# Block-sparse attention with top-2 experts: score products paired the other way round, and the row maximum carried by one transposed tile and a row copy

## Chip, cores and metric

One Trainium2 core of a chip with eight. The metric is the device time of one execution in microseconds (us); lower is better. Three executions of the kernel before took 1046.15, 1049.36 and 1059.47 us.

## What is computed

The reference first computes attention for 4 batches x 8 heads, 768 positions, head size 64, under a mask of blocks of 32 positions (neighbours, first and last block, three sampled blocks for each block of queries). Its rows then go through a top-2 mixture of 8 experts. Cut to what matters here:

```python
scores = 0.125 * (q @ k.T)                 # for each batch and head
scores = where(mask, scores, -1e9)
scores = scores - scores.max(-1)
attn = exp(scores); attn = attn / (attn.sum(-1) + 1e-9)
x = attn @ v                               # then rows of all heads, 3072 x 512
# router, top 2 of 8 experts, relu(x @ w1[e]) @ w2[e]
```

## The kernel before

The attention half (class Attention) runs over 32 heads, two heads to a group g, 16 groups. The 768 positions are T = 6 tiles of 128. A step n is one tile of 128 keys of one head (192 steps): `exp(n, x)` makes the scores of 128 keys against 384 queries (x = 0, 1) in PSUM and takes their exponential on ACT (L257), `halve` rescales them on DVE (L262), and `av`, three steps later, multiplies them with v on PE (L288).

q and k are 32-bit and are used as a sum of two 16-bit halves, a high part (qh, kh) and the remainder (ql, kl). A score is kh qh + kl qh + kh ql. Two products of up to 128 rows give it, and the rows above the first 64 carry the rest of the arithmetic:

- L255: `k1` (rows kh, kl) with `q1` (rows qh, qh).
- L256: `k2` (rows kh, 24 rows of the mask, two rows of the constant 64) with `q2` (rows ql, 24 rows eh that say in which block a query lies, a row -m/64, a constant row).

The row maximum m is needed ahead of the exponential. `max_mm` (L227) multiplies the upper part of `q3` (qh, eh) with `k2` (kh, mask), 88 rows, and `max_red` (L234) reduces on DVE. This work runs up to 11 steps ahead of the exponentials. When the last tile of a head is reduced, `max_end` writes -m/64 into the tile qb (L241, DVE) and one step later (`Q2LATE`) SP issues the transpose of the head's whole qb, six blocks of 128x128, into `q2` (L243).

The operands of a group are prepared two groups ahead by `split`, in the order of the table SPLITAT: casts of k and q to the high parts on ACT (L192, L196), remainders on POOL a step later (L194, L198), the transposes of ka (k1) and qa (q3) on SP at steps 5 and 6 of the 12 steps of a group (L181), the copy of kh from k1 to k2 at step 8 (L205), and two copies of qh from q3 to both halves of q1 at step 9 (L208, L209). The mask and constant rows of k2 never change: they lie in three buffers that groups use in turn.

All transposes and these copies are DMAs issued by SP, which issues in program order and stops at the first one whose semaphore isn't reached. On the same queue go, for each group, a transpose of the group's attention rows for the router (L495, x to r_xT) and their way to DRAM (L497, x_rows). ACT issues the loads of q, k and v (L160) and, in steps 20 to 48, eight stores of zeros over the output (L988, 768 KB each). The prologue `start` does the same for group 0 with SP transposes of each head, and the masks are built by `masks`, `blank` and `blocks`.

After the attention come the expert products, which the change doesn't touch.

Of the kernel before, what the change touches and what calls it, by code (L numbers as in the profile page):

```python
# [10 lines left out]
F16 = mybir.dt.float16  # L11
# [8 lines left out]
P = 128  # L20
# [24 lines left out]
class Attention:  # L45
# [27 lines left out]
    def open(self, ctx, early):  # L73

        tc, nc, G, T = self.tc, self.nc, self.G, self.T
        pool = lambda c, name, bufs, **kw: c.enter_context(tc.tile_pool(name=name, bufs=bufs, **kw))
        self.const = pool(ctx, "aconst", 1, side="right")
        self.tp = pool(ctx, "atp", 3, side="right")
        self.pp = pool(ctx, "app", self.PPB, side="right")
        self.pi = pool(ctx, "api", 3, side="right")  # L80
        self.sm = pool(ctx, "asm", 4, side="right")
        self.xp = pool(ctx, "axp", 2, side="right")
        self.ps_e = pool(ctx, "ps_e", 3, space=PSUM)
        self.ps_m = pool(ctx, "ps_m", 2, space=PSUM)
        self.ps_o = pool(ctx, "ps_o", 1, space=PSUM)
        self.natp = pool(ctx, "anat", 1, side="right")
        self.raw = pool(early, "araw", 2)
        self.nat = [tuple(self.natp.tile([P, G, T, P], F16, name=f"{n}{i}") for n in ("ka", "qa", "qb"))
                    for i in range(2)]
        self.k2 = [self.natp.tile([P, G, T, P], F16, name=f"k2{i}") for i in range(3)]  # L90

        self.vx = [self.natp.tile([P, G, T, self.D + 1], F16, name=f"vx{i}") for i in range(3)]
        self.vb = [self.natp.tile([P, G, T, self.D + 1], F16, name=f"vb{i}") for i in range(3)]
        self.vl = [self.natp.tile([P, G, T, self.D], F16, name=f"vl{i}") for i in range(3)]
        for t, w in zip(self.vx + self.vb, [VS / XS] * 3 + [VS / XS * LOW] * 3):
            nc.gpsimd.memset(t[:, :, :, self.D:], w)

    def masks(self, mi, sb):
# [9 lines left out]
        self.kb = mi.tile([P, G, T, P], F16, name="kb")  # L108
        nc.gpsimd.memset(self.kb[:, :, :, 64:], 0.0)
        nc.gpsimd.memset(self.kb[:, :, :, 64 + NB:66 + NB], 64.0)  # L110
        self.blank(0)
        nc.vector.tensor_scalar(rowi, rowi, 5, None, op0=ALU.arith_shift_right)
        rowb = mi.tile([P, T], F32, name="rowb")
        nc.vector.tensor_copy(rowb, rowi)
        rb = rowb[:, :, None].to_broadcast([P, T, NB])
        eh = mi.tile([P, T, NB], F32, name="eh")
        nc.vector.tensor_tensor(eh, bc(ei, NB), rb, op=ALU.is_equal)
        self.eh = eh
        self.blocks(0, 1)
        t1 = mi.tile([P, T, NB], F32, name="t1")  # L120
        nc.vector.tensor_tensor(t1, bc(ei, NB), rb, op=ALU.subtract)
        al = mi.tile([P, T, NB], F32, name="al")
# [15 lines left out]
            nc.vector.tensor_tensor(al, al, t3[:, :, j], op=ALU.add)  # L138
        for g in range(G):
            nc.vector.tensor_scalar(self.kb[:, g, :, 64:64 + NB], al, 0.0, -BIG, op0=ALU.is_equal, op1=ALU.mult)  # L140

    def blank(self, i):
        ka, qa, qb = self.nat[i]
        self.nc.gpsimd.memset(qa[:, :, :, 64 + self.NB:], 0.0)
        self.nc.gpsimd.memset(qb[:, :, :, 64 + self.NB:], 0.0)
        self.nc.gpsimd.memset(qb[:, :, :, 65 + self.NB:66 + self.NB], LNROW)

    def blocks(self, i, k):
        for g in range(self.G):
            self.nc.vector.tensor_scalar(self.nat[i][k][:, g, :, 64:64 + self.NB], self.eh, 2.0 ** 15, None, op0=ALU.mult)  # L150

    def load(self, g, eng=None, names="kq"):
        b, h0 = divmod(g * self.G, self.H)
# [30 lines left out]
    def split(self, g, part, h=None):  # L184

        nc, D, G, T = self.nc, self.D, self.G, self.T
        r = self.st[g]
        ka, qa, qb = self.nat[g % 2]
        kx, qx = r["k"], r["q"]
        hs = slice(0, G) if h is None else slice(h, h + 1)  # L190
        if part == 0:
            nc.scalar.activation(ka[:, hs, :, 0:D], kx[:, hs], AF.Copy)  # L192
            self.later(1 if self.now else 0,
                       lambda: nc.gpsimd.tensor_sub(ka[:, hs, :, D:], kx[:, hs], ka[:, hs, :, 0:D]))  # L194
        elif part == 1:
            nc.scalar.activation(qa[:, hs, :, 0:D], qx[:, hs], AF.Copy)  # L196
            self.later(1 if self.now else 0,
                       lambda: nc.gpsimd.tensor_sub(qb[:, hs, :, 0:D], qx[:, hs], qa[:, hs, :, 0:D]))  # L198
        elif part == 2:
            self.xpose(r, "k1", ka)  # L200
        elif part == 3:
            self.xpose(r, "q3", qa)
        elif part == 4:
            r["k2"] = self.k2[g % 3]
            nc.sync.dma_start(r["k2"][0:D], r["k1"][0:D])  # L205
        elif part == 5:
            q1 = self.new(r, "q1")
            nc.sync.dma_start(q1[0:D], r["q3"][0:D])  # L208
            nc.sync.dma_start(q1[D:], r["q3"][0:D])  # L209

    def where(self, n):
        hh, i = divmod(n, self.T)
# [6 lines left out]
    def max_mm(self, n):  # L219
        g, h, t = self.where(n)  # L220
        r = self.st[g]
        K = 64 + self.NB
        if t == 0:
            r["m", h] = self.sm.tile([P, self.T], F32, name="m")
        pm = self.ps_m.tile([P, 2, 512], F32, name="pm")
        for c in range(2):
            self.nc.tensor.matmul(pm[:, c, 0:384], r["q3"][0:K, h, t, :], r["k2"][0:K, h, 3 * c:3 * c + 3, :],  # L227
                                  start=True, stop=True)
        self.st["pm", n] = pm

# [5 lines left out]
    def max_end(self, n):  # L236
        g, h, t = self.where(n)
        r = self.st[g]
        if t == self.T - 1:
            qb = self.nat[g % 2][2]  # L240
            self.nc.vector.tensor_scalar(qb[:, h, :, 64 + self.NB], r["m", h], -1.0 / 64.0, None, op0=ALU.mult)  # L241
            d = r["q2", h] = self.tp.tile([P, self.T, P], F16, name="q2", bufs=2)
            self.later(self.Q2LATE, lambda: self.nc.sync.dma_start_transpose(  # L243
                out=d, in_=qb[:, h].rearrange("p t c -> p (t c)")))

    def exp(self, n, x):
        nc, T = self.nc, self.T
        g, h, c = self.where(n)
        r = self.st[g]
        if x == 0:  # L250
            self.st["p32", n] = self.pi.tile([P, T, P], I32, name="p32")
        p32 = self.st["p32", n]
        t = slice(3 * x, 3 * x + 3)
        pe = self.psum()
        nc.tensor.matmul(pe[:, 0:384], r["k1"][:, h, c, :], r["q1"][:, h, t, :], start=True, stop=False)  # L255
        nc.tensor.matmul(pe[:, 0:384], r["k2"][:, h, c, :], r["q2", h][:, t, :], start=False, stop=True)  # L256
        nc.scalar.activation(p32[:, t].rearrange("p t c -> p (t c)"), pe[:, 0:384], AF.Exp, scale=0.125)  # L257

    def halve(self, n):
# [61 lines left out]
    def start(self, mi):  # L321
# [7 lines left out]
            for nm, src in (("k", self.k), ("q", self.q)):  # L329
                nc.sync.dma_start(r[nm][:, h], src[0, h].rearrange("(p t) d -> p t d", p=P))  # L330
        self.masks(mi, sb)
        ka, qa, qb = self.nat[0]
        q3, k1 = self.new(r, "q3"), self.new(r, "k1")
        r["k2"] = self.k2[0]
        turn = lambda dst, src, h: nc.sync.dma_start_transpose(out=dst[:, h], in_=src[:, h].rearrange("p t c -> p (t c)"))
        for h in range(self.G):
            nc.scalar.activation(qa[:, h, :, 0:D], r["q"][:, h], AF.Copy)
            nc.scalar.activation(self.kb[:, h, :, 0:D], r["k"][:, h], AF.Copy)
            turn(q3, qa, h)
            turn(r["k2"], self.kb, h)  # L340
            self.load(1, nc.sync, "kq"[h])
        for h in range(self.G):
            nc.scalar.activation(ka[:, h, :, 0:D], r["k"][:, h], AF.Copy)
            nc.vector.tensor_sub(ka[:, h, :, D:], r["k"][:, h], ka[:, h, :, 0:D])
            nc.vector.tensor_sub(qb[:, h, :, 0:D], r["q"][:, h], qa[:, h, :, 0:D])
        nc.sync.dma_start_transpose(out=k1.rearrange("p g t c -> p (g t) c"), in_=ka.rearrange("p g t c -> p (g t c)"))
        self.blocks(0, 2)
        self.split(0, 5)
        self.blank(1)
        for n in range(self.T + self.XM):  # L350
            self.max_mm(n)
            self.max_red(n)
            if n in (self.S0, self.S0 + 1):
                self.split(1, n - self.S0)
            if n == self.S0:
                self.blocks(1, 1)
            self.max_end(n)
        self.flush()
        self.load(0, nc.scalar, "v")
        for i in range(3):  # L360
            self.vsplit(0, i)
        self.split(1, 3)
        self.split(1, 2)
        nc.sync.dma_start(self.k2[1][D:], self.k2[0][D:])
        self.split(1, 4)
        self.split(1, 5)
        self.blocks(1, 2)
        self.nmax = self.T + self.XM
        self.plan = {0: [(self.load, 2)], 3: [(self.load, 1, None, "v")], 4: [(self.load, 3)],
                     6: [(nc.sync.dma_start, self.k2[2][D:], self.k2[0][D:])]}  # L370

    def lead(self, n):
        return min(self.LM, self.T + 1 + max(0, self.NSTEP - n))
# [282 lines left out]
class Experts:  # L656
# [193 lines left out]
    def turn(self, u, c):  # L850
        m = self.rows_of(u, c)
        py = self.ps_r.tile([P, 512], F32, name="pr")
        for d in range(self.KB):
            self.nc.tensor.transpose(py[0:m, d * P:(d + 1) * P], self.yt[:, d, 0:m], self.router.ident)
        self.finish(u, c, py)
# [280 lines left out]
```

## Time and profile before

| | |
|---|---|
| median of three runs | 1049.36 us (1046.15 to 1059.47) |
| the profiled execution | 1054.67 us, its span 1052.9 us |
| mean granted clock of PE | 0.957 |
| PE busy | 897.5 us, 85% of the span |
| DVE busy | 549.4 us, 52% |
| ACT busy | 372.8 us, 35% |
| POOL busy | 340.9 us, 32% |
| DMA read and written | 156.40 MB, SP's and POOL's and ACT's queues together |
| transposes of qb, qa, ka on SP | 32, 17 and 16 |
| copies inside SBUF on SP, 192 KB each | 32 for q, 17 for k |

A line of the profile names an engine, an operation, the tiles it writes and reads, its count, its busy time and mean duration, and the idle time of the engine just ahead of it with what ended that idle time. A row of the order of time begins with its start and its duration in us. For a DMA, the row is its issue on the queue of SP or ACT; when it has landed is seen only by who waited for it. The share of DMA is that of the 16 DMA engines and can come out a little over 1.

### The profile page before, as it was taken

To read this page: it belongs to the slowest core of one execution; us is meant where nothing else is said; L and a number is where in the kernel's file an instruction comes from. 1 tells how busy PE (TensorE), PEld (TensorE's weight loads), DVE (VectorE), ACT (ScalarE), POOL (GpSimd) and SP (SyncE) were. 2 spreads that over 40 slices of the span, in tenths; PEclk is the share of its full clock that TensorE was granted. 3 is DMA by queue.
4 is the path that set the end of the run, shared out by engine and by line. 5 is a ranking of instruction groups with operands and counts; after the bars stand their busy time and mean duration, and the time that the engine had idled before them with its cause. 6 is when DMAs were issued, how large, how long until landed. Compare 5 with 4: busy or idle time off the path is not lost. (4 is left out here: it accounts for less than half of the span.)

```text
span 1052.9 us, 20575 instructions
## 1 busy us (share of the span) xinstructions
PE 897.5 (85%) x8413; PEld 531.8 (51%) x8413; DVE 549.4 (52%) x1039; ACT 372.8 (35%) x754; POOL 340.9 (32%) x399
## 2 busy tenths in 40 slices
PE   3887798888888768897797989979989999899993
PEld 1554565566566535654554445535545554454551
DVE  8787779999998945554134134133243251251220
ACT  3565556666666525432033032121131140230200
POOL 3232222552363342253360241331422422602211
PEclk9999999999999978998898999989999999999997
DMA  8999987788798518745959186194293392661200
GB/s 188 183 203 220 226 185 166 167 161 159 150 175 167 115 30 204 178 119 145 210 156 223 61 220 150 65 232 120 91 222 114 103 240 95 175 143 51 64 33 33
DMA packets 238073, 156.40 MB, mean 149 GB/s; under 512 B 172577, under 2 KB 213793, under 8 KB 237968
## 3 DMA queue, kind: packets, MB, share of 16 engines
q1 hardware_dynamic: 206816, 91.45, 42.8%
q0 software_dynamic: 14256, 39.58, 13.4%
q10 hardware_dynamic: 16896, 23.95, 8.3%
q8 instruction: 68, 1.11, 0.5%
q14 instruction: 37, 0.30, 0.1%
HBM read 79.62 MB, written 26.32 MB: 101 GB/s over the span
## 5 line engine op out<-in xcount | busy, mean ns | idle before, releaser
L257 ACT ACTIVATE p<-pe 128x384 int32<-128x384 f32 x384 | 182.4, 492 | 155.2 <-PE pe L256 128.1
L820 ACT ACTIVATE hh<-ph 128x408 f16<-128x408 f32 (+2 forms) x136 | 66.9, 493 | 378.9 <-PE ph L815 270.8
L234 DVE TENSOR_REDUCE m<-pm 128x1 f32<-128x768 f32 x192 | 181.9, 950 | 1.4 <-PE pm L227 1.4
L865 POOL DMA_INDIRECT out_dram<-y,mt x56 | 59.8, 1067 | 350.6 <-DVE y L863 258.5
L821 DVE SCALAR_TENSOR_TENSOR hl<-ph,hh 128x408 f16<-128x408 f32 (+2 forms) x136 | 76.1, 560 | 175.7 <-ACT hh L820 134.4
L227 PE MATMUL pm<-k,q 88*128 88x384 f16 x384 | 99.3, 343 | 65.3 <-DVE m L234 38.0
L262 DVE TENSOR_SCALAR p<-p 128x1536 f16<-128x1536 uint16 x192 | 115.6, 602 | 62.8 <-ACT p L257 49.7
L288 PEld LDWEIGHTS <-p 128*128 128x128 f16 x3456 | 131.6, 100 | 27.6 <-issue 6.8
L255 PE MATMUL pe<-q,k 128*128 128x384 f16 x384 | 129.8, 338 | 13.0 <-ACT p L257 6.3
L256 PE MATMUL pe<-q,k 128*128 128x384 f16 x384 | 129.1, 336 | 8.4 <-DMA q<-qb 8.2
L863 DVE SCALAR_TENSOR_TENSOR y<-py,mt,pv 128x512 f32<-128x512 f32 x48 | 36.0, 751 | 189.8 <-PE py L835 181.3
L288 PE MATMUL po<-vl,p 128*128 128x64 f16 x1152 | 126.4, 196 | 1.9 <-issue 1.9
L288 PE MATMUL po<-vb,p 128*128 128x65 f16 x1152 | 126.6, 197 | 1.5 <-issue 1.5
L288 PE MATMUL po<-vx,p 128*128 128x65 f16 x1152 | 126.2, 198 | 0.5 <-DVE p L262 0.4
L815 PE MATMUL ph<-xta,w1hb 128*128 128x408 f16 x512 | 112.4, 342 | 15.7 <-DVE hl L821 13.2
L835 PEld LDWEIGHTS <-hh 128*128 128x128 f16 x768 | 75.0, 98 | 92.1 <-issue 6.9
L815 PE MATMUL ph<-xtb,w1ha 128*128 128x408 f16 (+1 forms) x448 | 97.1, 337 | 21.6 <-DVE hl L821 16.5
L227 PEld LDWEIGHTS <-q 88*128 88x128 f16 x384 | 37.9, 100 | 120.4 <-issue 94.1
L815 PEld LDWEIGHTS <-w1ha 128*128 128x128 f16 x576 | 57.7, 101 | 61.7 <-issue 28.1
L815 PEld LDWEIGHTS <-w1hb 128*128 128x128 f16 x512 | 50.8, 99 | 57.2 <-issue 20.9
L835 PE MATMUL py<-w2ha,hh 128*128 128x512 f16 x192 | 73.8, 384 | 3.6 <-DVE y L863 3.6
L835 PE MATMUL py<-w2ha,hl 128*128 128x512 f16 x192 | 73.8, 384 | 1.7 <-issue 1.7
(172 smaller groups left out, 1398.7 us busy)
## 6 DMA issues: line engine op xcount, KB each, us to landing
wraw<-in_moe_w_dram SPq DMA_DIRECT2D x64, 512.0 KB
q<-q SPq DMA_DIRECT2D x32, 192.0 KB
raw_v<-in_v_dram ACTq DMA_DIRECT2D x16, 384.0 KB
out_dram<-zero ACTq DMA_DIRECT2D x8, 768.0 KB
x_rows<-x SPq DMA_DIRECT2D x16, 384.0 KB
raw_k<-in_k_dram ACTq DMA_DIRECT2D x14, 384.0 KB
raw_q<-in_q_dram ACTq DMA_DIRECT2D x14, 384.0 KB
k<-k SPq DMA_DIRECT2D x17, 192.0 KB
```

The lines of the kernel that those rows point to most:

```text
L227: self.nc.tensor.matmul(pm[:, c, 0:384], r["q3"][0:K, h, t, :], r["k2"][0:K, h, 3 * c:3 * c + 3, :], start=True, stop=True)
L234: self.nc.vector.tensor_reduce(self.st[g]["m", h][:, t:t + 1], pm[:, :, 0:384], axis=AX.XY, op=ALU.max)
L255: nc.tensor.matmul(pe[:, 0:384], r["k1"][:, h, c, :], r["q1"][:, h, t, :], start=True, stop=False)
L256: nc.tensor.matmul(pe[:, 0:384], r["k2"][:, h, c, :], r["q2", h][:, t, :], start=False, stop=True)
L257: nc.scalar.activation(p32[:, t].rearrange("p t c -> p (t c)"), pe[:, 0:384], AF.Exp, scale=0.125)
L262: self.nc.vector.tensor_scalar(p.rearrange("p t c w -> p (t c w)"), p32.bitcast(U16).rearrange("p t c -> p (t c)"), HC, None, op0=ALU.mult)
L288: self.nc.tensor.matmul(o, p[:, t, :, w], v, start=first and i == 0, stop=last and i == 2, skip_group_check=True)
L815: nc.tensor.matmul(ph[:, b, 0:m], w[wt][:, kb, fs], r["xt"][:, kb, a, o:o + m], start=i == 0, stop=i == last)
L820: nc.scalar.activation(hv, ph[:, b, 0:m], AF.Relu)
L821: nc.vector.scalar_tensor_tensor(self.hl[:, f, o:o + m], ph[:, b, 0:m], 0.0, hv, op0=ALU.max, op1=ALU.subtract)
L835: nc.tensor.matmul(py, h[:, f, o], w[x][:, f, :], start=i == 0, stop=i == last)
L865: nc.gpsimd.indirect_dma_start(out=self.out, out_offset=bass.IndirectOffsetOnAxis(ap=r["mt"][0:m, c, 0:1], axis=0), in_=y[0:m], in_offset= ...
```

## The change

- The first product becomes (kh, kl) with (ql, qh): one transpose of the tile qn (ql, qh) gives `q1`, and both copies of qh into it go.
- The second becomes (kh, mask, 64) with (qh, eh, -m): `q2` now holds qh, copied from the lower half of q1 (one copy), over constant rows that are kept in three buffers as those of k2 are. The maximum is taken from q2 instead of q3, which goes. The product contracts over 90 rows instead of 128.
- -m/64 is written into the first six columns of a small tile `mn`. SP transposes this one 128x128 block, and a second DMA copies its six rows into row 88 of q2 (one partition).
- The prologue follows: its q transposes go straight into q2, k1 and q1 are two transposes of 12 blocks, and the constant rows of q2 are copied into the other two buffers as those of k2 are.

```diff
-        self.nat = [tuple(... for n in ("ka", "qa", "qb")) for i in range(2)]
+        self.nat = [tuple(... for n in ("kn", "qn")) for i in range(2)]
+        self.q2 = [self.natp.tile([P, G, T, P], F16, name=f"q2{i}") for i in range(3)]
+        self.mn = [self.natp.tile([P, P], F16, name=f"mn{i}") for i in range(3)]
...
-        if part == 0:
-            nc.scalar.activation(ka[:, hs, :, 0:D], kx[:, hs], AF.Copy)
+        if part < 2:
+            src, dst, hi, lo = ((kx, kn, slice(0, D), slice(D, None)), (qx, qn, slice(D, None), slice(0, D)))[part]
+            nc.scalar.activation(dst[:, hs, :, hi], src[:, hs], AF.Copy)
             self.later(1 if self.now else 0,
-                       lambda: nc.gpsimd.tensor_sub(ka[:, hs, :, D:], kx[:, hs], ka[:, hs, :, 0:D]))
-        elif part == 1:
-            nc.scalar.activation(qa[:, hs, :, 0:D], qx[:, hs], AF.Copy)
-            self.later(1 if self.now else 0,
-                       lambda: nc.gpsimd.tensor_sub(qb[:, hs, :, 0:D], qx[:, hs], qa[:, hs, :, 0:D]))
+                       lambda: nc.gpsimd.tensor_sub(dst[:, hs, :, lo], src[:, hs], dst[:, hs, :, hi]))
         elif part == 2:
-            self.xpose(r, "k1", ka)
+            self.xpose(r, "k1", kn)
         elif part == 3:
-            self.xpose(r, "q3", qa)
+            self.xpose(r, "q1", qn)
...
         elif part == 5:
-            q1 = self.new(r, "q1")
-            nc.sync.dma_start(q1[0:D], r["q3"][0:D])
-            nc.sync.dma_start(q1[D:], r["q3"][0:D])
+            r["q2"] = self.q2[g % 3]
+            nc.sync.dma_start(r["q2"][0:D], r["q1"][D:])
...
-            self.nc.tensor.matmul(pm[:, c, 0:384], r["q3"][0:K, h, t, :], r["k2"][0:K, h, 3 * c:3 * c + 3, :],
+            self.nc.tensor.matmul(pm[:, c, 0:384], r["q2"][0:K, h, t, :], r["k2"][0:K, h, 3 * c:3 * c + 3, :],
...
-            qb = self.nat[g % 2][2]
-            self.nc.vector.tensor_scalar(qb[:, h, :, 64 + self.NB], r["m", h], -1.0 / 64.0, None, op0=ALU.mult)
-            d = r["q2", h] = self.tp.tile([P, self.T, P], F16, name="q2", bufs=2)
-            self.later(self.Q2LATE, lambda: self.nc.sync.dma_start_transpose(
-                out=d, in_=qb[:, h].rearrange("p t c -> p (t c)")))
+            mn = self.mn[(n // self.T) % 3]
+            self.nc.vector.tensor_scalar(mn[:, 0:self.T], r["m", h], -1.0 / 64.0, None, op0=ALU.mult)
+            self.later(self.Q2LATE, lambda: self.max_row(g, h, mn))
+
+    def max_row(self, g, h, mn):
+        NB, T = self.NB, self.T
+        mt = self.tp.tile([P, P], F16, name="mt", bufs=2)
+        self.nc.sync.dma_start_transpose(out=mt, in_=mn)
+        self.nc.sync.dma_start(self.st[g]["q2"][64 + NB:65 + NB, h], mt[0:T, :])
...
-        nc.tensor.matmul(pe[:, 0:384], r["k2"][:, h, c, :], r["q2", h][:, t, :], start=False, stop=True)
+        K = 66 + self.NB
+        nc.tensor.matmul(pe[:, 0:384], r["k2"][0:K, h, c, :], r["q2"][0:K, h, t, :], start=False, stop=True)
...
-        nc.sync.dma_start(self.k2[1][D:], self.k2[0][D:])
+        for t in (self.k2, self.q2):
+            nc.sync.dma_start(t[1][D:], t[0][D:])
...
-                     6: [(nc.sync.dma_start, self.k2[2][D:], self.k2[0][D:])]}
+                     6: [(nc.sync.dma_start, t[2][D:], t[0][D:]) for t in (self.k2, self.q2)]}
```

More of the change, by code (lines that the diff above doesn't have):

```diff
@@ L87, in open @@
         self.raw = pool(early, "araw", 2)
-        self.nat = [tuple(self.natp.tile([P, G, T, P], F16, name=f"{n}{i}") for n in ("ka", "qa", "qb"))
+        self.nat = [tuple(self.natp.tile([P, G, T, P], F16, name=f"{n}{i}") for n in ("kn", "qn"))
                     for i in range(2)]
         self.k2 = [self.natp.tile([P, G, T, P], F16, name=f"k2{i}") for i in range(3)]
+        self.q2 = [self.natp.tile([P, G, T, P], F16, name=f"q2{i}") for i in range(3)]
+        self.mn = [self.natp.tile([P, P], F16, name=f"mn{i}") for i in range(3)]
+        for t in self.mn:
+            nc.gpsimd.memset(t, 0.0)
         self.vx = [self.natp.tile([P, G, T, self.D + 1], F16, name=f"vx{i}") for i in range(3)]
@@ L110, in masks @@
         nc.gpsimd.memset(self.kb[:, :, :, 64 + NB:66 + NB], 64.0)
-        self.blank(0)
+        self.qb = mi.tile([P, G, T, P], F16, name="qb")
+        nc.gpsimd.memset(self.qb[:, :, :, 64 + NB:], 0.0)
+        nc.gpsimd.memset(self.qb[:, :, :, 65 + NB:66 + NB], LNROW)
         nc.vector.tensor_scalar(rowi, rowi, 5, None, op0=ALU.arith_shift_right)
@@ L117, in masks @@
         nc.vector.tensor_tensor(eh, bc(ei, NB), rb, op=ALU.is_equal)
-        self.eh = eh
-        self.blocks(0, 1)
+        for g in range(G):
+            nc.vector.tensor_scalar(self.qb[:, g, :, 64:64 + NB], eh, BIG, None, op0=ALU.mult)
         t1 = mi.tile([P, T, NB], F32, name="t1")
@@ L140, in masks @@
             nc.vector.tensor_scalar(self.kb[:, g, :, 64:64 + NB], al, 0.0, -BIG, op0=ALU.is_equal, op1=ALU.mult)
[L142 to L150, printed above, removed]
     def load(self, g, eng=None, names="kq"):
@@ L187, in split @@
         r = self.st[g]
-        ka, qa, qb = self.nat[g % 2]
+        kn, qn = self.nat[g % 2]
         kx, qx = r["k"], r["q"]
         hs = slice(0, G) if h is None else slice(h, h + 1)
-        if part == 0:
-            nc.scalar.activation(ka[:, hs, :, 0:D], kx[:, hs], AF.Copy)
+        if part < 2:
+            src, dst, hi, lo = ((kx, kn, slice(0, D), slice(D, None)), (qx, qn, slice(D, None), slice(0, D)))[part]
+            nc.scalar.activation(dst[:, hs, :, hi], src[:, hs], AF.Copy)
             self.later(1 if self.now else 0,
-                       lambda: nc.gpsimd.tensor_sub(ka[:, hs, :, D:], kx[:, hs], ka[:, hs, :, 0:D]))
-        elif part == 1:
-            nc.scalar.activation(qa[:, hs, :, 0:D], qx[:, hs], AF.Copy)
-            self.later(1 if self.now else 0,
-                       lambda: nc.gpsimd.tensor_sub(qb[:, hs, :, 0:D], qx[:, hs], qa[:, hs, :, 0:D]))
+                       lambda: nc.gpsimd.tensor_sub(dst[:, hs, :, lo], src[:, hs], dst[:, hs, :, hi]))
         elif part == 2:
-            self.xpose(r, "k1", ka)
+            self.xpose(r, "k1", kn)
         elif part == 3:
-            self.xpose(r, "q3", qa)
+            self.xpose(r, "q1", qn)
         elif part == 4:
@@ L331, in start @@
         self.masks(mi, sb)
-        ka, qa, qb = self.nat[0]
-        q3, k1 = self.new(r, "q3"), self.new(r, "k1")
-        r["k2"] = self.k2[0]
+        kn, qn = self.nat[0]
+        kb, qb = self.kb, self.qb
+        r["k2"], r["q2"] = self.k2[0], self.q2[0]
         turn = lambda dst, src, h: nc.sync.dma_start_transpose(out=dst[:, h], in_=src[:, h].rearrange("p t c -> p (t c)"))
         for h in range(self.G):
[L337 to L340, printed above, removed]
+            nc.scalar.activation(qb[:, h, :, 0:D], r["q"][:, h], AF.Copy)
+            nc.scalar.activation(kb[:, h, :, 0:D], r["k"][:, h], AF.Copy)
+            turn(r["q2"], qb, h)
+            turn(r["k2"], kb, h)
             self.load(1, nc.sync, "kq"[h])
         for h in range(self.G):
[L343 to L349, printed above, removed]
+            nc.scalar.activation(kn[:, h, :, 0:D], r["k"][:, h], AF.Copy)
+            nc.vector.tensor_sub(kn[:, h, :, D:], r["k"][:, h], kb[:, h, :, 0:D])
+            nc.scalar.activation(qn[:, h, :, D:], r["q"][:, h], AF.Copy)
+            nc.vector.tensor_sub(qn[:, h, :, 0:D], r["q"][:, h], qb[:, h, :, 0:D])
+        self.xpose(r, "k1", kn)
+        self.xpose(r, "q1", qn)
         for n in range(self.T + self.XM):
@@ L354, in start @@
                 self.split(1, n - self.S0)
-            if n == self.S0:
-                self.blocks(1, 1)
             self.max_end(n)
@@ L363, in start @@
         self.split(1, 2)
-        nc.sync.dma_start(self.k2[1][D:], self.k2[0][D:])
+        for t in (self.k2, self.q2):
+            nc.sync.dma_start(t[1][D:], t[0][D:])
         self.split(1, 4)
         self.split(1, 5)
-        self.blocks(1, 2)
         self.nmax = self.T + self.XM
         self.plan = {0: [(self.load, 2)], 3: [(self.load, 1, None, "v")], 4: [(self.load, 3)],
-                     6: [(nc.sync.dma_start, self.k2[2][D:], self.k2[0][D:])]}
+                     6: [(nc.sync.dma_start, t[2][D:], t[0][D:]) for t in (self.k2, self.q2)]}
     def lead(self, n):
```

## The prediction

> **What bounds the kernel now.** I read the page first (span, the DMA slices), then busy time by stretch, then the groups of instructions inside a stretch, then the order of time around single waits.
>
> ```profile
> span 1052.9 us, 20575 instructions
> ...
> DMA  8999987788798518745959186194293392661200
> ```
>
> The slices are 26 us each: the DMA engines are full in the first six and seldom later. The attention half is slices 0 to 15; the change touches nothing after it. I cut it into a front, a stretch in which the output is also filled with zeros, and a steady stretch.
>
> ```profile
> 22.41:66.27 43.86, 36.46 (x453) 23.66 (x452) 35.25 (x59) 25.04 (x55) 14.34 (x21) 0.96 1.01 185
> 66.27:146.41 80.14, 62.19 (x867) 43.15 (x866) 59.50 (x102) 44.87 (x101) 19.52 (x21) 0.94 1.06 223
> 146.41:343.84 197.43, 168.26 (x2608) 118.41 (x2607) 182.58 (x379) 126.48 (x289) 83.09 (x107) 1.00 0.82 162
> ```
>
> Columns: length, busy PE, PEld, DVE, ACT, POOL, granted clock, DMA share, GB/s. In the first two rows DMA is at 1.01 and 1.06, no engine above 83%. In the third DVE is busy 182.58 of 197.43 us (92%) and DMA 0.82. So **DMA bounds up to about 146 us, and DVE (with PE close) after it**. The groups of the second and third stretch say what the DMA costs:
>
> ```profile
> L257 ACT ACTIVATE p<-pe 128x384 int32<-128x384 f32 x73 | 34.9, 492 | 36.2 <-PE pe L256 33.3 <-PE pm L227 2.1 <-DVE m L234 0.2
> ...
> L256 PE MATMUL pe<-q,k 128*128 128x384 f16 x73 | 24.5, 335 | 6.8 <-DMA q<-qb 6.8
> ...
> L227 PE MATMUL pm<-k,q 88*128 88x384 f16 x73 | 18.6, 336 | 10.7 <-DMA k<-k 6.1 <-DVE m L234 4.6
> ```
>
> ```profile
> L257 ACT ACTIVATE p<-pe 128x384 int32<-128x384 f32 x205 | 97.7, 492 | 70.2 <-PE pe L256 59.3 <-PE pm L227 6.2 <-DVE r_mx L560 1.8
> ...
> L227 PE MATMUL pm<-k,q 88*128 88x384 f16 x204 | 49.7, 324 | 29.2 <-DVE m L234 22.0 <-issue 3.2 <-DMA k<-k 2.0
> ```
>
> A step has two exponentials (L257). In the fill stretch 73 of them take 80.14 us, 1.098 us each; steady, 205 take 197.43 us, 0.963 us each. At the steady pace the 73 would take 70.3 us, so the stretch loses 9.8 us, and PE's two DMA waits there add up to 12.9 us: for the late transpose that carries -m (6.8) and for the copy of kh (6.1). In the steady stretch only 2.0 us of such waits are left.
>
> **The change part by part.** For each group of two heads, TRANSPOSES go from 12 (k) + 12 (q) + 2 x 6 (ql with -m) blocks of 128x128 to 12 + 12 + 2 x 1; 192 KB COPIES from three (kh, and qh twice) to two (kh, qh); two 1.5 KB row copies are new. I price a block where a 12-block transpose is alone, and plain bytes where a zero fill runs:
>
> ```profile
> 258.30:260.30 2.00, 0.48 (x8) 0.19 (x5) 2.00 (x4) 1.25 (x3) 1.51 (x2) 1.00 1.03 195
> 69.50:70.50 1.00, 0.87 (x12) 0.60 (x12) 1.00 (x5) 0.15 (x2) 0.00 (x0) 1.00 1.07 416
> ```
>
> A block is 32.8 KB, at 195 GB/s 0.168 us of all 16 engines; 196.6 KB at 416 GB/s is 0.47 us. Saved in each group: 10 x 0.168 + 0.47 = 2.15 us.
>
> *Fill stretch.* 73 exponentials are three groups (24 each), so 6.5 us of DMA time goes. While DMA is the bound this comes off the time: **-6.5**. Bounds: 0 (the waits stay latencies) and -9.8 (the steady pace, where DVE is late next).
>
> The row is also faster here than the transpose it replaces:
>
> ```profile
> 76.28 3.10 SPq L243 DMA_TRANSPOSE q<-qb  x1
> ...
> 86.11 5.81 SPq L181 DMA_TRANSPOSE q<-qa  x1
> ```
>
> ```profile
> 87.33 0.32 PE L256 MATMUL pe<-q,k 128*128 128x384 f16 x1 [1.66 <-DMA q<-qb]
> ...
> 100.44 0.32 PE L256 MATMUL pe<-q,k 128*128 128x384 f16 x1 [2.74 <-DMA q<-qb]
> ```
>
> Under load the six blocks took 11 us from issue (76.28) to use (87.33); one block has a sixth of the packets to get through the same crowd.
>
> *Front.* The first head shows both kinds of transfer with little beside them:
>
> ```profile
> 19.12 1.21 SPq L243 DMA_TRANSPOSE q<-qb  x1
> ...
> 29.42 0.46 SPq L205 DMA_DIRECT2D k<-k  x1
> ```
>
> ```profile
> 21.90 0.48 PE L256 MATMUL pe<-q,k 128*128 128x384 f16 x1 [1.42 <-DMA q<-qb]
> ...
> 32.23 0.81 PE L227 MATMUL pm<-k,q 88*128 88x384 f16 x4 [2.21 <-DMA k<-k]
> ```
>
> Six blocks: 19.12 to 21.90 = 2.78 us. One block: five blocks less, 2.78 - 0.84 = 1.94. A copy: 29.42 to 32.23 = 2.81, without the bytes' 0.47 it is 2.34. No row shows a 1.5 KB copy; it lies between its issue alone (0.46) and 2.81, and I take 2.34, the same kind on the same queue. The row then needs 4.28 us instead of 2.78: +1.5 on the first head (bounds -0.4 and +2.8). SP waits inside this chain, since the row copy may only be issued when the block has landed: SP is free at 19.12 + 1.94 + 0.46 = 21.5 instead of 20.3. Behind it stand the next group's two transposes, the constant rows (two copies now, 0.5 more) and the copies of kh and, new on the way of the row maximum, qh; that adds up to 2.3 us at the maximum that started at 32.23, 1.5 of it the same delay. Against it the front's four heads and two groups move 20 blocks and two copies less and one constant copy more, 3.8 us of DMA time at a share of 1.01; I count half. Front: +2 - 1.9, **0** (-4 to +4).
>
> The Trainium skill (DMA: Bandwidth & Descriptors, Anatomy of one DMA) speaks against this part: a semaphore wait is spent in the issuing sequencer before dispatch, and a DMA has a fixed cost of about 2 us, fitted there for the GpSimd path. By it the two in a row would cost about 4 us as an estimate, +1.2 instead of my +1.5; the 2.78 us row agrees, no row yet shows SP waiting inside a pair.
>
> *Steady stretch.* Each group's SP order after its odd head:
>
> ```profile
> 194.35 1.21 SPq L243 DMA_TRANSPOSE q<-qb  x1
> 195.66 1.50 SPq L495 DMA_TRANSPOSE r_xT<-x  x1
> 197.21 0.92 SPq L497 DMA_DIRECT2D x_rows<-x  x1
> 198.23 0.63 SPq L205 DMA_DIRECT2D k<-k  x1
> 198.91 1.00 SPq L208 DMA_DIRECT2D q<-q  x1
> 199.96 1.87 SPq L209 DMA_DIRECT2D q<-q  x1
> ```
>
> ```profile
> 204.08 0.48 PE L227 MATMUL pm<-k,q 88*128 88x384 f16 x2 [1.03 <-DMA k<-k]
> ```
>
> The copy of kh is already just in time: issued 198.23, used 204.08 after a wait of 1.03. After the change the row copy holds SP to 194.35 + 1.94 + 0.46 = 196.75, so the transpose of x, x_rows and the kh copy move by 1.1 us, and the maximum also needs the qh copy, 0.67 later. If issue decides, the maximum is late by 1.1 + 0.67 = 1.77 us. If the end of the burst decides (5.85 us from issue to use say so, against 2.81 alone), it is 1.1 - 0.47 = 0.63, or -0.2 where the five missing blocks count. I take 0.63, the longer latency being the nearest row. Eight groups; some have DVE work that hides it, I charge six: **+4** (bounds -2, the two waits gone, and 8 x 1.77 = +14). The row itself has five steps, 5 x 2 x 0.963 = 9.6 us, for 4.28.
>
> *At nothing.* The second product contracts over 90 rows instead of 128: above, 88 rows cost 336 ns and 128 rows 335. Casts, remainders and the scaling of m keep their number. The q transpose now waits for POOL's remainder as well as for the cast:
>
> ```profile
> 81.59 0.91 POOL L198 TENSOR_TENSOR qb<-raw_q,qa 128x384 f16<-128x384 f32 x1 [2.48 <-ACT qa L196]
> 87.80 0.92 POOL L198 TENSOR_TENSOR qb<-raw_q,qa 128x384 f16<-128x384 f32 x1 [5.29 <-DMA q<-qb]
> ```
>
> That is 0.9 us, hidden in the gap of SP ahead of the next -m, and POOL's 5.29 us wait goes, because no late transpose reads that tile any more. The prologue's fills and block constants change places under the wait for q and k.
>
> **Sum:** -6.5 + 0 + 4 = -2.5 us. The profiled execution took 1054.67 us (span 1052.9), 5.3 above the median 1049.36 of runs from 1046.15 to 1059.47; 2.5 off it is 1052.2, and off the median 1047. Less than 2% either way (21 us) can hardly be told from no change here.
>
> **The rivals.**
> 1. *The crowd clears altogether*: fill stretch at the steady pace (-9.8), front -4, steady waits gone (-2): -16, **1033**. For it: the shares of 1.01 and 1.06. Against: the kh and qh copies now wait behind a held SP. Chance 0.22.
> 2. *Late copies, warm clock*: issue decides, +14 steady, +2 front, the fill gain -6.5 kept: **1059**. Chance 0.11.
> 3. *Late copies make PE cold* (the slower one): a wait of 1.03 + 1.77 = 2.8 us at every group's first maximum. The 2.74 us wait at 100.44 was followed by this:
>
> ```profile
> 100.00:110.00 10.00, 8.63 (x91) 5.89 (x91) 3.29 (x6) 4.33 (x10) 1.83 (x2) 0.66 1.11 220
> ```
>
> Ten us at a clock of 0.66 lose 3.4 us. Eight groups x (1.77 + 3.4) = +41, with -6.5: **1084**. It decides from an added lateness of about 1.7 us; at 0.63 the wait is 1.7 us and the clock stays, as after 1.03. Chance 0.08. The Trainium skill (TensorE: Matmul & The Clock Gate, What's actually happening) puts the fall to half clock at an idle window of about 3.4 us; by it 2.8 us would be mostly safe, and the 2.74 us row says it need not be.
> 4. *The row write blocks other heads*: if a write to one row of a head made the products of the other head wait, each of 32 heads would stop for up to 4.28 us: +137, **1186**. Against: the remainder of 81.59 ran while the transpose of the other head's half of that tile (76.28 to 87.33) was under way. Chance 0.03.
>
> **How the numbers follow.** Forecast 1047 (1040 to 1056): 0.56. Faster by over 2%: 0.04, since even rival 1 stays inside. Slower by over 2%: rivals 3 and 4 and a little of 2, 0.12. Same: 0.84. The range 1033 to 1064 holds the forecast, rival 2 and the half of rival 1 above its own figure.
>
> **What would show it.** Right: the fill stretch's exponentials near 1.0 us each, its DMA wait at the second product gone, 26 instead of 36 blocks a group, the steady maximum waiting 1 to 2 us for the qh copy at a clock of 1.00. Wrong: a clock below 0.9 between 150 and 340 us, PE waiting for the row copy at each head's first exponential, or the fill stretch still at 1.1 us with DMA below 1.

## The result and the profile after

| | median, us | range, runs | the profiled execution | span |
|---|---|---|---|---|
| before | 1051.55 | 1046.15 to 1059.47, 4 | 1054.67 | 1052.9 |
| after | 1083.26 | 1079.01 to 1091.62, 4 | 1080.75 | 1078.9 |

The ratio is 1.0305 with an interval of 1.021 to 1.0401: **slower**, by 32 us where 2.5 less was forecast. The same kernel beside other runs (e9 below) came out at 1.0217 (1.0152 to 1.0283).

First the page of the kernel after: span and DMA slices (27 us each).

```profile
span 1078.9 us, 20587 instructions
...
DMA  7669865776555524954859367177186293561200
```

Of the first six slices one is still full of DMA (9), and the kernel is slower all the same. The same three stretches, cut where ACT begins to copy out the sums of heads 2, 8 and 25, say where. Busy time by stretch, kernel after; columns as before:

```profile
22.41:71.93 49.52, 40.66 (x454) 25.84 (x454) 33.86 (x57) 25.06 (x56) 14.27 (x21) 1.00 0.66 155
71.93:146.62 74.69, 63.98 (x867) 43.97 (x866) 59.67 (x102) 45.26 (x102) 20.01 (x21) 0.91 0.85 218
146.62:365.11 218.49, 179.00 (x2608) 124.15 (x2607) 182.40 (x379) 127.39 (x290) 82.72 (x107) 0.95 0.63 126
```

| us | up to head 2 | fill | steady | the rest |
|---|---|---|---|---|
| before | 66.27 | 80.14 | 197.43 | 709.1 |
| after | 71.93 (+5.7) | 74.69 (-5.5) | 218.49 (+21.1) | 713.8 (+4.7) |

The granted clock of 1.00 in the first row can't be used: this trace has no clock record before 45.20 us (the front is taken up again below). Front and fill cancel: head 8 is reached at 146.62 instead of 146.41. The loss is the steady stretch, where DVE's work is the same (182.40 us against 182.58) but PE is busy 10.7 us longer for the same 2608 matmuls, at a clock of 0.95 instead of 1.00, and the DMA share has fallen from 0.82 to 0.63. The groups of instructions there, kernel after:

```profile
L254 ACT ACTIVATE p<-pe 128x384 int32<-128x384 f32 x205 | 97.9, 490 | 90.4 <-PE pe L253 82.7 <-PE pm L219 3.2 <-DVE r_z L521 1.7
L253 PE MATMUL pe<-q,k 90*128 90x384 f16 x205 | 68.8, 336 | 3.3 <-DMA q<-mt 3.3
...
L219 PE MATMUL pm<-k,q 88*128 88x384 f16 x204 | 52.1, 338 | 36.2 <-DVE m L226 18.9 <-DMA q<-q 14.7 <-issue 1.8
```

PE's wait for the copy that the maximum needs was 2.0 us (kh, L227); now it is 14.7 us, for qh (L219), and the row adds 3.3. The waits for DVE shrink by 3.1 (22.0 to 18.9). PE's idle time grows by 10.3 us in all (29.2 to 39.5); with the 10.7 us of slower matmuls that is the 21.1. SP's order of time around one group says why (start, duration):

```profile
297.98 1.97 SPq L239 DMA_TRANSPOSE mt<-mn  x1
302.17 0.73 SPq L240 DMA_DIRECT2D q<-mt  x1
303.01 1.44 SPq L489 DMA_TRANSPOSE r_xT<-x  x1
304.50 0.92 SPq L491 DMA_DIRECT2D x_rows<-x  x1
305.53 0.61 SPq L198 DMA_DIRECT2D k<-k  x1
306.19 0.86 SPq L201 DMA_DIRECT2D q<-q  x1
```

Between the one-block transpose and its row copy SP stands still, 4.19 us from issue to issue, and four DMAs stand behind it. The copy of kh goes out 7.55 us after the transpose; in the group shown of before it was 198.23 - 194.35 = 3.88. SP's list of waits sums it up (times, longest):

```profile
SPq L240 <- DMA mt<-mn: 50.9, 28, 4.6
```

What follows on PE, in order of time:

```profile
306.40 0.33 PE L253 MATMUL pe<-q,k 90*128 90x384 f16 x1
310.16 0.82 PE L219 MATMUL pm<-k,q 88*128 88x384 f16 x2 [3.43 <-DMA q<-q]
310.77 0.53 PE L251 MATMUL pe<-q,k 128*128 128x384 f16 x1
```

PE waits 3.43 us for qh, and then a product of 384 columns takes 0.53 us instead of 0.33. The ten us around it, and ten others with waits of 2.65 (for the row) and 2.16 us (for qh):

```profile
308.00:318.00 10.00, 7.66 (x78) 5.18 (x79) 3.65 (x8) 3.93 (x9) 3.42 (x5) 0.66 0.61 149
204.00:214.00 10.00, 5.27 (x76) 3.61 (x76) 4.84 (x8) 3.88 (x9) 3.35 (x5) 1.00 0.53 118
```

So a late qh can cost twice: the wait, and a stretch of matmuls at half clock (here called cold) beside it. Five waits for qh in the steady stretch are over 1 us: those before 157.15, 235.05, 310.16 and 337.11 (1.19, 2.97, 3.43 and 3.39 us) come with half clock, for 3.41, 3.41, 6.83 and 6.83 us by the trace's clock records; the one of 2.16 doesn't. A fifth cold piece of 3.41 us follows a wait for DVE (1.58 us, before 270.73).

### The profile page after: what moved, and what is told of

It is laid out like the page before. It is cut to its first block, busy times and chain, and to the rows that moved or that the text cites. A ratio compares the mean times of both kernels' runs of the same rounds, so it can differ in the third digit from the quotient of the medians.

```text
span 1078.9 us, 20587 instructions
## 1 busy us (share of the span) xinstructions
PE 915.9 (85%) x8413; PEld 541.5 (50%) x8413; DVE 546.1 (51%) x1033; ACT 374.4 (35%) x756; POOL 338.6 (31%) x398
## 5 line engine op out<-in xcount | busy, mean ns | idle before, releaser
L219 PE MATMUL pm<-k,q 88*128 88x384 f16 x384 | 104.6, 358 | 69.5 <-DVE m L226 33.5
L285 PEld LDWEIGHTS <-p 128*128 128x128 f16 x3456 | 137.1, 102 | 33.3 <-issue 13.0
L251 PE MATMUL pe<-q,k 128*128 128x384 f16 x384 | 134.0, 349 | 10.0 <-ACT p L254 5.4
L253 PE MATMUL pe<-q,k 90*128 90x384 f16 x384 | 133.7, 348 | 8.5 <-DMA q<-mt 7.3
L285 PE MATMUL po<-vx,p 128*128 128x65 f16 x1152 | 131.3, 200 | 4.4 <-issue 4.0
L285 PE MATMUL po<-vb,p 128*128 128x65 f16 x1152 | 131.2, 200 | 1.5 <-issue 1.5
L285 PE MATMUL po<-vl,p 128*128 128x64 f16 x1152 | 130.9, 199 | 1.7 <-issue 1.6
L809 PE MATMUL ph<-xtb,w1ha 128*128 128x408 f16 (+1 forms) x448 | 99.6, 342 | 24.0 <-DVE hl L815 14.3
L219 PEld LDWEIGHTS <-q 88*128 88x128 f16 x384 | 38.9, 104 | 127.6 <-issue 76.7
L829 PE MATMUL py<-w2la,hh 128*128 128x512 f16 x192 | 73.4, 382 | 0.3 <-issue 0.3
```

The lines of the kernel that those rows point to most:

```text
L219: self.nc.tensor.matmul(pm[:, c, 0:384], r["q2"][0:K, h, t, :], r["k2"][0:K, h, 3 * c:3 * c + 3, :], start=True, stop=True)
L253: nc.tensor.matmul(pe[:, 0:384], r["k2"][0:K, h, c, :], r["q2"][0:K, h, t, :], start=False, stop=True)
L285: self.nc.tensor.matmul(o, p[:, t, :, w], v, start=first and i == 0, stop=last and i == 2, skip_group_check=True)
L809: nc.tensor.matmul(ph[:, b, 0:m], w[wt][:, kb, fs], r["xt"][:, kb, a, o:o + m], start=i == 0, stop=i == last)
L829: nc.tensor.matmul(py, h[:, f, o], w[x][:, f, :], start=i == 0, stop=i == last)
```

## The experiments

**Theory H**: the row copy holds SP until the small transpose has landed; what stands behind it (the copies of kh and qh) comes late, PE waits and cools. **Rivals**: the writes into one row of q2 block other work; the maximum's new dependence on qh alone is at fault; the extra DMAs cost by their number. The chips differ: beside e1 to e4 the kernel before took 1053.74 us, beside e5 to e8 1013.41 (another chip, where the part after the attention half takes 664 to 676 us, against 708 to 717 in the other runs), beside e9 to e12 1052.25. Ratios are compared.

**e1: the row copy one step later.** SP goes on with the transpose of x and x_rows while the block lands; the row copy still stands ahead of kh and qh.

```diff
-        self.nc.sync.dma_start(self.st[g]["q2"][64 + NB:65 + NB, h], mt[0:T, :])
+        self.later(1 if self.now else 0, lambda: self.nc.sync.dma_start(self.st[g]["q2"][64 + NB:65 + NB, h], mt[0:T, :]))
```

> The changed kernel with the row copy issued one step after its transpose, behind the transpose of x and x_rows, so that SP isn't held for the block to land. Held-queue theory (the pair of dependent DMAs holds SP, so the copies of kh and qh behind it come late): the steady stretch goes back from 218 to about 200 us, the waits for the qh copy shrink to 1 us or less, time about 1065 us (the front's extra 6 us stay). Qh-dependency theory (the maximum is late because it needs one more copy than before): the copies stay late by 0.7 us and the time stays at 1078 to 1083. Row-latency theory (the row itself lands too late): the row lands 2 us later still, its waits grow, 1085 to 1100.

Measured 1066.7 us, ratio 1.0141 (1.0063 to 1.022). Busy time in the steady stretch, and PE's waits:

```profile
148.53:354.58 206.05, 173.28 (x2608) 121.67 (x2607) 182.82 (x379) 126.62 (x290) 82.87 (x107) 0.98 0.64 133
```

```profile
PE pe L253 <- DMA q<-mt: 20.0, 8, 4.3
```

PE's waits for qh have gone and the stretch is 12.4 us shorter than after's, but now the row is late. kh goes out 4.5 to 5.2 us after the transpose, where the change had 5.6 to 8.6. Only the order on SP was changed, so the order is a cause; the maximum needs qh here as it does in the change, so that need alone is not. And there is no slack on the row to pay with.

**e2: the row copy from a constant tile**, which waits for nothing; the row maximum stays out of the scores. Both DMAs are still issued.

```diff
+        self.rowc = self.natp.tile([P, P], F16, name="rowc")
...
-        self.nc.sync.dma_start(self.st[g]["q2"][64 + NB:65 + NB, h], mt[0:T, :])
+        self.nc.sync.dma_start(self.st[g]["q2"][64 + NB:65 + NB, h], self.rowc[0:T, :])
```

> The changed kernel with the row copy taken from a constant tile instead of the transposed one, so that it waits for nothing (left out: the row maximum, the row is zero); the one-block transpose is still issued and the same bytes move. Held-queue theory: steady stretch near 200 us, and the front gains the transpose's latency too, about 1060 us. Qh-dependency theory: 1078 to 1083. Row-latency theory: about 1065, with no wait for the qh copy removed.

Measured 1056.92 us, ratio 1.0079 (1.0028 to 1.0131). SP's order of time, the busy time of the steady stretch and PE's wait for qh there (a line later in this kernel):

```profile
193.58 1.12 SPq L240 DMA_TRANSPOSE mt<-mn  x1
194.76 0.74 SPq L241 DMA_DIRECT2D q<-rowc  x1
195.60 1.46 SPq L490 DMA_TRANSPOSE r_xT<-x  x1
```

```profile
145.40:346.79 201.39, 169.00 (x2608) 118.77 (x2607) 182.31 (x379) 126.73 (x290) 82.80 (x107) 1.00 0.67 136
```

```profile
PE pm L220 <- DMA q<-q: 5.7, 3, 2.4
```

Issue to issue falls to 1.18 us and the clock is 1.00 again. The stretch keeps 4.0 us over before's 197.43, and qh is not always in time even without the hold: its 5.7 us are 3.7 more than before's wait for kh. In the fill stretch the waits for qh stay as they were (7.0 us, 6.4 after the change), so there they are not the hold's. The same row of q2 is written, so the rival of the row write falls.

**e3: the kernel before with the pair added**, its result into a tile that nobody reads.

```diff
+        self.mn = self.natp.tile([P, P], F16, name="mn")
+        self.spare = self.natp.tile([P, T, P], F16, name="spare")
...
-            self.later(self.Q2LATE, lambda: self.nc.sync.dma_start_transpose(
-                out=d, in_=qb[:, h].rearrange("p t c -> p (t c)")))
+            self.later(self.Q2LATE, lambda: (self.nc.sync.dma_start_transpose(
+                out=d, in_=qb[:, h].rearrange("p t c -> p (t c)")), self.pair()))
+    def pair(self):
+        mt = self.tp.tile([P, P], F16, name="mt", bufs=2)
+        self.nc.sync.dma_start_transpose(out=mt, in_=self.mn)
+        self.nc.sync.dma_start(self.spare[88:89], mt[0:self.T, :])
```

> The kernel before, with a one-block transpose and a dependent row copy into a tile nobody reads, issued behind each late transpose of a head. It adds the hold of SP and nothing that anyone waits for. Held-queue theory: the waits for the kh copy grow from 2 us to 15 us or more in the steady stretch, time 1070 to 1080. Qh-dependency theory and row-latency theory: 1051 to 1056, the DMA time of 32 blocks (5 us) in the crowded stretch at most.

Measured 1097.96 us, ratio 1.0477 (1.0392 to 1.0562). The steady stretch, PE's waits and SP's:

```profile
157.73:382.47 224.74, 178.15 (x2608) 123.19 (x2607) 183.42 (x379) 126.86 (x289) 82.64 (x107) 0.95 0.74 146
```

```profile
PE pm L230 <- DMA k<-k: 43.2, 13, 7.6
```

```profile
SPq L252 <- DMA mt<-mn: 88.2, 30, 5.6
```

Nobody depends on the pair's data, and yet PE waits 43.2 us for kh (10.3 in the whole of before), 20.4 of them in the steady stretch (2.0), and the clock falls to the same 0.95. The time is above the 1070 to 1080 that theory H gave. The hold of SP costs without any of the new pairing, and SP waits longer where the small transpose stands behind the large one (88.2 us against 50.9).

**e4: the maximum without qh.** It multiplies rows of ql with kh, so the mask and qh stay out of it and it is no maximum of the scores.

```diff
-            self.nc.tensor.matmul(pm[:, c, 0:384], r["q2"][0:K, h, t, :], r["k2"][0:K, h, 3 * c:3 * c + 3, :],
+            self.nc.tensor.matmul(pm[:, c, 0:384], r["q1"][0:64, h, t, :], r["k2"][0:64, h, 3 * c:3 * c + 3, :],
```

> The changed kernel with the maximum taken from the product of ql (out of q1) with kh (out of k2), so that it does not wait for the qh copy but still for the kh copy (another product than the score is maximised, the mask is left out of it). Held-queue theory: the kh copy is issued only 0.7 us ahead of the qh copy and is as late because of the hold, so only some 5 us come back: 1075 to 1080. Qh-dependency theory: all of the steady loss comes back, 1060 to 1065.

Measured 1083.48 us, ratio 1.035 (1.0248 to 1.0452): in its total **inconclusive**, since the edit brought costs of its own. A wait of PE, then the steady stretch and the product for the maximum in it:

```profile
PE pm L219 <- DMA q<-qn: 21.0, 1, 21.0
```

```profile
159.75:367.35 207.60, 186.40 (x2608) 106.48 (x2608) 183.32 (x379) 129.37 (x289) 82.42 (x107) 0.98 0.65 132
```

```profile
L219 PE MATMUL pm<-k,q 64*128 64x384 f16 x205 | 50.9, 328 | 19.2 <-DVE m L226 13.1 <-DVE mn L233 3.0 <-DMA k<-k 1.9
```

The 21.0 us are one wait, of the first head for the transpose of q1, and head 2 comes 9.7 us later than in after (81.66). The steady stretch alone gives back 10.9 of the 21.1 us (207.60). SP is held as before (62.1 us), but kh, issued just ahead of qh, is hardly late: 1.9 us of waits in the place of qh's 14.7. So in the steady stretch the hold seems to cost by way of qh, the later copy. How much belongs to each is not settled: PE is busy 7.4 us longer here than in the changed kernel, at a higher clock, and that too gives the copies time.

**e5: the row copy issued by POOL's queue** instead of SP's.

```diff
-        self.nc.sync.dma_start(self.st[g]["q2"][64 + NB:65 + NB, h], mt[0:T, :])
+        self.nc.gpsimd.dma_start(self.st[g]["q2"][64 + NB:65 + NB, h], mt[0:T, :])
```

> The changed kernel with the row copy issued from POOL instead of SP: POOL waits for the block to land, SP goes straight on to the transpose of x and the copies of kh and qh. Held-queue theory: the qh waits of the steady stretch go as they did with the later row copy, and the row itself isn't late behind x_rows either, so better than that kernel: 1055 to 1062. Theory that two dependent DMAs are late in the crowd whoever issues them: the waits for the row stay near 20 us as with the later copy, 1066. POOL as the new bound (it waits 2 to 5 us for each head with remainders and indirect DMAs behind it): above 1075.

Measured 1063.8 us, ratio 1.0537 (1.0463 to 1.0611): worse than the change, and the expectation failed. Waits of POOL and PE:

```profile
POOL q L240 <- DMA mt<-mn: 130.9, 20, 10.6
...
PE pe L253 <- DMA q<-mt: 30.2, 16, 6.3
```

The hold is not gone, it has moved: POOL, which makes the remainders of q and k, now stands still 130.9 us, and the row comes later still.

**e6, e7, e8: the copies issued earlier.** The table SPLITAT is moved up, so that kh and qh are issued at step 6 of a group, ahead of the pair: in the changed kernel (e6), in the kernel before (e7), and with e5's POOL copy (e8).

```diff
-    SPLITAT = ((0, 0, 0), (1, 0, 1), (2, 1, 0), (5, 1, 1), (5, 2, None), (6, 3, None), (8, 4, None), (9, 5, None))
+    SPLITAT = ((0, 0, 0), (1, 0, 1), (2, 1, 0), (3, 1, 1), (4, 2, None), (5, 3, None), (6, 4, None), (6, 5, None))
```

> The changed kernel with the pair left on SP, but with the second half's cast of q two steps earlier, the transposes of k and q at steps 4 and 5 and the copies of kh and qh at step 6, ahead of the row pair instead of behind it. Held-queue theory: only the router's transpose and x_rows stand behind the held SP, the qh waits vanish, the steady stretch is 198 us or less, 1055 to 1062. If it is the late copies that matter and not what holds them, the same. If the row pair's own latency is what costs (rows late in the crowd), the gain is under 10 us.

> The kernel before with the same earlier table of splits, as the measure for the one before. Its kh copies were just in time and PE waited 10 us for them in all, with cold stretches behind two of the waits: 1043 to 1051 if the earlier copies take these away; 1053 if DVE bounds anyway.

> Both: row copy on POOL and the early table of splits. Held-queue theory: nothing is left to wait for the pair but the first head, 1050 to 1058, and with the smaller DMA traffic the crowded stretch keeps its 5 us gain. If it isn't below the early table alone, the hold was already harmless there.

Measured: e6 1033.3 us, 1.0192 (1.012 to 1.0264); e7 1004.83 us, 0.9938 (0.9893 to 0.9984); e8 1069.83 us, 1.0596 (1.0511 to 1.0681). Waits of PE in e6, then the steady stretch of e6 and that of e7:

```profile
PE pe L253 <- DMA q<-mt: 31.5, 15, 4.3
```

```profile
149.83:356.12 206.29, 174.95 (x2608) 123.04 (x2607) 176.16 (x379) 127.20 (x289) 83.11 (x107) 0.96 0.61 132
```

```profile
147.94:339.67 191.73, 168.01 (x2608) 118.64 (x2606) 180.41 (x379) 127.38 (x290) 83.54 (x107) 1.00 0.81 164
```

In e6 the waits for qh are gone and the row is late instead, 15 times: the two chains share one queue, and moving one ahead makes the other late. The stretch stays above the 198 us that was expected. e8 failed its expectation too: PE waits 47.2 us for the row there and POOL stands still for 130.6. The kernel before takes the same table as a gain; e7 is the only complete kernel here that is below both, 0.6% below the kernel before.

**e9: the changed kernel again**, unedited.

> The changed kernel once more, beside the next three on one chip: 1.03 times the kernel before, steady stretch 218 us, as measured the first time, whatever the theory.

1081.06 us, ratio 1.0217; its steady stretch is 218.30 us against 218.49.

**e10, e11: the row sooner too.** e10 is e6 with the transpose of the row issued in the step of its scaling; e11 also runs the maximum one step further ahead.

```diff
-    Q2LATE = 1
+    Q2LATE = 0
...
-        self.LM = self.T + 5
+        self.LM = self.T + 6        # e11 alone
```

> The early table of splits, and the row pair issued in the same step in which the head's maximum ends instead of one step later. What is left of the loss with the early table alone is 31 us of waits for the row. Row-latency theory (the pair takes some 7 us in the crowd, not 4.3, and misses its head): one step of 2 us more takes most of the 1.6 to 4.3 us waits away, 0.5 to 1.5% off the early table alone, ratio to before 1.005 to 1.015. If the waits only move along with the row, ratio 1.02 as without it.

> As the one before, and the maxima run one step further ahead (12 instead of 11), so the row has two steps more in all. Row-latency theory: no wait for the row is left but the first head's 4 us; with the lighter DMA traffic ratio 0.99 to 1.005. A bound elsewhere (DVE, the front): the same as with one step.

e10: 1070.08 us, 1.0167 (1.0121 to 1.0213), PE's waits for the row down to 19.9 us, a smaller gain than expected. e11: 1088.31 us, 1.037 (1.03 to 1.0439); here the expectation failed. PE's waits and SP's order of time in e11:

```profile
PE pm L219 <- DMA q<-q: 37.2, 11, 5.2
...
PE pe L253 <- DMA q<-mt: 5.1, 2, 4.1
```

```profile
202.29 1.13 SPq L239 DMA_TRANSPOSE mt<-mn  x1
205.05 0.73 SPq L240 DMA_DIRECT2D q<-mt  x1
205.83 1.33 SPq L177 DMA_TRANSPOSE q<-qn  x1
207.28 1.04 SPq L198 DMA_DIRECT2D k<-k  x1
211.91 0.51 SPq L201 DMA_DIRECT2D q<-q  x1
```

The row is in time, but the pair now stands ahead of the q transpose and of both copies, and qh is late again. Neither order of the two chains served both.

**e12: no row DMAs.** The transposed tile and its row copy are left out, and so is the row maximum from the scores; the pairing stays.

```diff
-        mt = self.tp.tile([P, P], F16, name="mt", bufs=2)
-        self.nc.sync.dma_start_transpose(out=mt, in_=mn)
-        self.nc.sync.dma_start(self.st[g]["q2"][64 + NB:65 + NB, h], mt[0:T, :])
+        pass
```

> The changed kernel without the row's transpose and copy (left out: the row maximum; the row keeps its constant). What the new pairing alone does. Held-queue and row-latency theories: all of the loss is gone and the lighter traffic shows, ratio 0.99 to 1.0, a little below the kernel with the row copied from a constant (1.008). If the pairing itself (the maximum behind the qh copy) costs: 1.01 or more.

Measured 1044.05 us, ratio 0.9904 (0.986 to 0.9949). Fill and steady stretch, and PE's longest sum of waits in the latter:

```profile
67.66:133.84 66.18, 58.20 (x867) 40.53 (x866) 59.55 (x102) 44.88 (x102) 20.03 (x21) 1.00 0.96 243
133.84:336.02 202.18, 174.27 (x2608) 122.51 (x2607) 182.85 (x379) 125.81 (x289) 83.02 (x107) 0.97 0.63 133
```

```profile
PE pm L219 <- DVE m L226: 25.6, 44, 1.6
```

Without any transport of -m the new pairing gains 1.0%, and more than all of it in the fill stretch (-14.0 us). A kernel that gives right results has to bring -m somehow, so this is a bound and no kernel. Against it, e2 (both DMAs, no hold) stands at 1.0079, and the whole change at 1.0305 or 1.0217. e2's profile is 7.5 us longer than e12's in the fill and 4.1 in the front, and not in the steady stretch (201.39 and 202.18 us). That both stay 4 to 5 us over before there has two reasons: in e2 PE waits for qh at full clock; in e12 it waits for no DMA, but is busy 6.0 us longer at a clock of 0.97, after waits for the maximum such as before has too (22.0 us). So what the pairing costs in this stretch is not shown. Across these runs, then, on different chips: pairing without -m -1.0%, the two DMAs of each head +1.8%, the hold another +1.4 to +2.3%.

## Why the prediction was wrong

*The failed step* is in the steady stretch: "If issue decides, the maximum is late by 1.77 us. If the end of the burst decides, it is 0.63. I take 0.63." The maximum was later than either, because the hold in front of the copies was mis-sized; and the term put the clock that follows a late copy at nothing. I had 1.94 us for the one-block transpose, from the six-block one with five blocks taken off, and 0.46 for the issue of the row copy. In the changed kernel issue to issue took 2.22 us at best, 2.7 in the median and up to 5.8, and the row copy's issue 0.74; after odd heads kh was issued 5.6 to 8.6 us after the transpose where before's steady groups have 3.8 to 4.5. Group by group that is +1.6 to +4.7 us for a term of +1.1, and qh goes out 0.7 us behind kh. A sixth of the packets is not a sixth of the time in a queue that has other packets ahead: my sentence that one block "has a sixth of the packets to get through the same crowd" was wrong. The steady term of +4 (bounds -2 to +14) came out at +21.1, 10.3 of it idle time of PE and 10.7 slower matmuls.

*Rival 3* had the mechanism: late copies, a PE that cools, decided from an added lateness of about 1.7 us. I gave it 0.08. Its total of 1084 is near the measured 1083, but not for its own sum: it had +41 in the steady stretch, which was +21.1, and nothing for the front (+5.7) and the rest (+4.7). The +41 were 14 of waits and 27 of cold clock, eight groups of 3.4 us. PE's waits for qh in the kernel after:

```profile
PE pm L219 <- DMA q<-q: 21.4, 11, 3.4
```

The steady stretch has 14.7 of these 21.4 us, 12.7 more than before's wait for kh, and so the size of the 14; but the cold part is 10.7 us instead of 27, because four groups and not eight had a wait for qh that came with half clock, two of them for 3.41 us only. Its price for ten us at a clock of 0.66 fits the row at 308. What did not hold is its condition, the length of the wait: the prediction left the clock alone at a wait of 1.7 us, and waits of 1.87 (before 107.19) and 1.19 us came with half clock. The Trainium skill (TensorE: Matmul & The Clock Gate, What's actually happening) puts the fall at an idle window of about 3.4 us. The trace agrees in part: the granted clock changes only at the edges of pieces of 3.41 us, but it fell at 308.03, when the 3.43 us wait was 1.3 us old. Such pieces, first the one with the wait of 2.74 us in the kernel before, then those at the waits of 2.65 and 3.43 us in the kernel after:

```profile
97.84:101.25 3.41, 0.81 (x5) 0.48 (x5) 1.76 (x3) 0.39 (x1) 0.48 (x1) 1.00 1.22 299
```

```profile
202.21:205.62 3.41, 1.71 (x26) 1.13 (x24) 3.31 (x7) 1.37 (x4) 0.91 (x1) 1.00 1.39 43
...
304.61:308.02 3.41, 1.83 (x25) 1.03 (x23) 3.38 (x6) 1.86 (x4) 1.59 (x4) 1.00 1.09 250
308.03:314.86 6.83, 4.70 (x45) 3.32 (x46) 1.44 (x3) 1.49 (x4) 1.81 (x2) 0.50 0.43 108
```

The 2.74 us wait lay nearly whole in one piece (PE busy 0.81 of 3.41 us), and half clock followed. The 2.65 us wait was spread over two pieces, and the clock stayed. So it seems to count where a wait lies, beside its length. That is still no rule: half clock followed a piece with 1.83 us of busy PE, and not one with 1.71.

*The front*, forecast at 0, was +5.7. Both rows of the first head, kernel after:

```profile
17.64 1.21 SPq L239 DMA_TRANSPOSE mt<-mn  x1
21.42 0.88 SPq L240 DMA_DIRECT2D q<-mt  x1
```

```profile
25.70 0.48 PE L253 MATMUL pe<-q,k 90*128 90x384 f16 x1 [4.04 <-DMA q<-mt]
```

The row copy took the 4.28 us from issue to use that I had for the pair together, on top of 3.78 for the block behind 24 others: 8.06 against 2.78 before. The row is used at 25.70 instead of 21.90, +3.8 where I had +1.5. The other 2 us are a PE that stays at half clock for longer. The first product of the exponentials from 34 to 46 us, in the kernel after and in the same kernel's e9:

```profile
L251 PE MATMUL pe<-q,k 128*128 128x384 f16 x7 | 3.4, 491 | 0.0
```

```profile
L251 PE MATMUL pe<-q,k 128*128 128x384 f16 x9 | 2.9, 327 | 0.0
```

From the first exponential of head 0 to that of head 1 it took 18.8 us here, 16.8 in e9 and 16.8 before; e9's front is 69.41, 3.1 over before. So the row is the part that repeats, and the rest differs from one execution to the next of the same kernel. e2, without the hold, has its first exponential at 21.90 (22.41 before), but half clock until 40.62 and again for 3.41 us from 64.51, and ends its front at 71.75. Why PE came to full clock late was not sought.

The Trainium skill (DMA: Bandwidth & Descriptors, Anatomy of one DMA) has some 2 us fixed for a DMA, fitted there for the GpSimd path, so an estimate of 4 for two; the traces agree with it as a floor alone, at 2.22 and 4.28 us. The Trainium skill's sentence there that a semaphore wait is spent in the issuing sequencer is what decided here, and SP's 50.9 us and POOL's 130.9 show it.

*Right* were the gone wait for the row in the fill stretch and the products over 90 rows at no change (336 ns). The fill stretch itself came out near the forecast (-5.5 against -6.5), in part by luck: e9 has 77.54 there, -2.6. My bound of -9.8 was too narrow: e12 shows -14.0, at 0.907 us for an exponential, so the steady pace was no floor. What kept the change from it is again PE, which waits 6.4 us for qh (6.1 for kh before) and has a clock of 0.91 in that stretch. Rival 4 was not seen: the row's waits are 7.3 us in all, 4 times. Rival 1 failed though the crowd did clear (a DMA share of 0.85 in the fill and 0.63 after it): the copies stood behind a held SP, as its own objection said.

The +4.7 us in the rest, after the changed half, are of the size by which the rest differs between e1 and e2 (717.3 and 707.8), and no cause was sought. Not tried was a way to get -m into one row of q2 without a DMA that depends on another DMA.

## What to carry to other kernels

A DMA that depends on another DMA of the same in-order queue is priced by what stands behind it: take the landing time under load, not the time by bytes, add it to every DMA that follows, and find the first consumer without that slack. Moving the dependent DMA to another queue moves the hold to that engine; moving it later only chooses who is late. Before giving up a wait-free transfer for fewer bytes, look whether the bytes are the bound in the stretch where most of the steps run.

## What the runs showed of the hardware that was not expected

- A transfer of 1.5 KB into one partition took longer from issue to use than a large one: 4.28 us in the front, with two 12-block transposes issued right behind it, where 192 KB took 2.81 in the kernel before.
- A one-block transpose gains little from its size behind others: 2.22 us from issue to the issue of the copy that waits for it at best, 3.78 behind 24 blocks, up to 5.8.
- A dependent DMA holds POOL as it holds SP, and there with longer single waits (10.6 us against 4.6).
- Half clock came with single waits of PE as short as 1.19 us (the clock fell at 157.84), and a wait of 2.65 us (to 206.57) left it at 1.00.
